# Fourteen opening matmuls, a last tile in three column pieces, and a re-ordered front of a linear-attention and channel-mix kernel

## The chip, the cores and the metric

The kernel runs on one core of a Trainium2 chip. The metric is the time on the device in microseconds (us) of one execution. Before the change it is 198.37 us, the median of three runs (198.21 to 198.51).

## What is computed

Eight batches of 576 tokens with 8 heads of 64 channels go through linear attention without a softmax, an RMS norm per head, and then a channel mix with two gates. The shapes are batch 8, 512 channels, and a hidden width of 1024.

```python
kv = einsum('bhsd,bhse->bhde', k, v)
y = einsum('bhsd,bhde->bhse', q, kv)
y = y / sqrt(mean(y*y, -1) + 1e-6) * g_norm
x = y.transpose(0, 2, 1, 3).reshape(B, S, H * D)
x_prev = x shifted by one token, zero at the first
xk = mu_k * x + (1 - mu_k) * x_prev
xr = mu_r * x + (1 - mu_r) * x_prev
k = max(xk @ w_k, 0)
out = sigmoid(xr @ w_r) * ((k * k) @ w_v)
```

Inputs and output are float32. The kernel works in bfloat16 on TensorE and accumulates in float32.

## The kernel before

The program is a list of steps, the string `ORDER` (lines 18 to 109), which a loop at the end of the kernel (line 685) walks word by word. Each word names a step and its arguments; every step issues its instructions at once to the engines that it uses. Each engine then works through its own instructions in that order, and waits where data or a buffer is not ready. So the order of `ORDER` is the order on every engine and on every DMA queue. A number behind `=` is the PSUM bank that the step's result takes; a mark `'` puts a step on VectorE (DVE) instead of ScalarE (ACT).

The steps that matter here:

- `wm.N` (line 252) issues N matmuls of zeros with 512 columns, whose result nobody reads. `wm.12` and `wm.7` open the program: 19 of them run before any other matmul. Shorter ones (`wm.1`, `wm.2`) stand between the front's steps.
- `lraw`, `lf`, `lw`, `ld` load. `lraw` (first two head pairs of k and v of batch 0) goes over SyncE's queue (SP), the others over the GpSimd queue (POOL), one behind the other: q of batch 0, the remaining k and v, q of batch 1, the four quarters of `w_k` (`lw.0.0` to `lw.0.3`), `w_r`, k and v of batch 1, two halves of `w_v`, and then the later batches. POOL issues a load only when the eighth load before it has landed.
- `cast` turns the raw k and v into bfloat16. `kc` (line 301) multiplies k with v for two batches with 64x64 matmuls; `kco` copies a product out of PSUM. `qc` (line 312) transposes q on TensorE, `qco` copies it out. `uc` (line 323) multiplies the transposed q with the product.
- `sq` squares on ACT (line 434), `ms` averages with a matmul (line 438), `rs` takes the reciprocal root on ACT (line 443), `mu` multiplies on DVE (line 462). That is the norm. `col` transposes the small vectors mu_k, mu_r and g_norm.
- `dc`, `sc`, `add`, `fu` blend x with the token before it.
- `Kf`, `Kl` (lines 530 and 541) are batch 0's matmuls with `w_k`, `Kfo`, `Klo`, `ksp` the relu and the square behind them. `K`, `Ko`, `ks` are the same for the later batches (line 555).
- `R` and `S` are the matmuls with `w_r` (line 575) and the sigmoid; `V` those with `w_v` (line 585), `fin` the last product on DVE (line 600), `st` the store on SP's queue (line 617).
- `tab` (line 647) loads ACT's table, either for the reciprocal root or for the sigmoid; a load blocks ACT.

The last tile, tile 8 of batch 7, has 128 tokens and 512 columns. `L.1` and `L.0` (line 593) compute its right and its left half of columns with eight matmuls each, `Lf` multiplies with the sigmoid on DVE, and `Ls` stores. Each half of columns is stored as two DMAs of 64 tokens: one on SP's queue and one on ACT's.

```python
    def store_half(n, part):
        ...
        (nc.sync, nc.scalar)[n].dma_start(out=dst[half(n), c], in_=o[half(n)])
```

At the end of the program SP waits, in nine instructions one behind the other, for the semaphores of all DMAs (each store's semaphore is one of eight that are given out in turn) before the engines meet and the kernel ends.

Of the kernel before, what the change touches and what calls it, by code (L numbers as in the profile page):

```python
# [21 lines left out]
    sq.0.0 col.1 qco.0.2.192.576' ms.0.1=2 rs.0.1 mu.0.1 qc.0.0.2.0.192=70 qco.0.0.0.192 ms.0.0=1 rs.0.0 mu.0.0  # L22
    kc.0.2.3=3 kco.0.2 wm.2=2 uc.0.2=2 sq.0.2 qco.0.3.192.576 lf.0.1.3.4.0.576 dc.0.0.2.256.576 lf.0.0.3.4.0.576
    kc.0.3.4=7 kco.0.3 wm.1=1 ms.0.2=1 rs.0.2 wm.1=6 uc.0.3=6 sq.0.3 uc.0.4=3 sq.0.4 sc.0.0.0.256.576'
    sc.0.0.1.256.576' qco.0.1.0.192' wm.1=5 uc.0.6=5 sq.0.6 add.0.0.0.256.576 mu.0.2 ms.0.3=4 rs.0.3 mu.0.3
    ms.0.4=7 rs.0.4 mu.0.4 wrap.0 uc.0.5=0 sq.0.5 ms.0.6=1 rs.0.6 dc.0.2.3.256.576 lf.1.2.0.4.0.576 wm.2=2
    qc.1.0.2.0.576=24 qco.1.1.0.576 qc.1.2.4.0.576=76 qco.1.3.0.576 fu.0.0.2.256.576 mu.0.6 dc.0.3.4.256.576
    ms.0.5=3 rs.0.5 qco.1.2.0.576 tab.1.0 fu.0.0.3.256.576 mu.0.5 dc.0.0.4.0.256 sc.0.0.0.0.256 sc.0.0.1.0.256
    lw.0.0.0.4.0.2 Kf.1.0.2.256=1 Kf.0.0.2.256=4 Kf.0.2.3.256 qco.1.0.0.576' lw.0.1.0.4.2.4 wm.2=6
    Kf.3.0.2.256=6 Kf.2.0.2.256=5 Kf.2.2.3.256 Kf.2.3.4.256 Kf.3.2.3.256 Kf.3.3.4.256 sc.0.1.0' sc.0.1.1'  # L30
    add.0.0.0.0.256 Kf.0.3.4.256 Kfo.0.256 lw.0.2.0.4.4.6 Kf.5.0.4.256=3 sc.0.0.3.0.256' Kfo.5.256
    Kf.4.0.4.256=7 lw.0.3.0.4.6.8 sc.0.1.2 Kf.6.0.4.256=0 Kf.7.0.4.256=2 sc.0.0.2.0.256' Kfo.6.256
    add.0.0.1.0.256 Kf.1.2.3.256 Kl.0.256=4 Kl.2.256=3 Klo.2.256 Kfo.7.256 sc.0.1.3' Kfo.4.256 lw.1.0.0.4.0.4
    lf.1.0.0.4.0.576 add.0.1.0 add.0.1.1 lf.1.1.0.2.0.576 R.0.2=0 S.0.2 Klo.0.256 Kf.1.3.4.256 ksp.4.8.256.576'
    R.0.3=3 S.0.3 Kfo.1.256' Kfo.2.256 Kfo.3.256' ksp.0.4.256.576' lf.1.1.2.4.0.576 R.0.1=2 S.0.1 R.0.0=7 S.0.0
# [77 lines left out]
def kernel(  # L113
# [605 lines left out]
```

## Time and profile before

| | us |
|---|---|
| median of three runs | 198.37 |
| range of the three runs | 198.21 to 198.51 |
| the profiled execution | 198.81 |
| its span, first to last instruction | 197.0 |
| TensorE (PE) busy, matmuls | 189.2, 96% of the span |
| ACT busy | 153.4, 78% |
| DVE busy | 150.0, 76% |

The page of the profile gives busy time of each engine, a chain of waits that follows the work back from the last instruction, the costliest groups of instructions, and the DMA issues with their median time to landing. PE's weight loads (PEld) run beside its matmuls. Matmuls overlap: a matmul's own duration is longer than its distance to the next one, so costs on PE are best taken from starts. In the timeline a bracket behind a row says how long the engine sat idle before it and what ended the wait. The DMA engines are busy at a share of 0.9 or more in nearly every slice of the first third of the span, and later more loosely.

### The profile page before, as it was taken

The page shows a single profiled execution, that of the slowest core. Times are in us where ns is not written, and L with a number is a line of the kernel's source. Part 1 is how long each engine was busy: PE and PEld are TensorE (multiplying, and loading weights), DVE is VectorE, ACT ScalarE, POOL GpSimd, SP SyncE. Part 2 cuts the span into 40 slices and gives each one's busy share as a digit, 9 for nine tenths or more (in the row PEclk, how much of TensorE's full clock was granted, in tenths as well). Part 3 has the DMA queues.
Part 4 walks back from the last instruction along what each step waited for, and adds up shares of the span by engine and source line. Part 5 has one row for each costly group of instructions (what it writes and reads, how often), then busy time and mean ns, then how long its engine had stood idle before and what let it go on. Part 6 is the DMA issues. An engine that isn't in the chain of part 4 may idle for free.

```text
span 197.0 us, 4744 instructions
## 1 busy us (share of the span) xinstructions
PE 189.2 (96%) x1879; PEld 111.4 (57%) x1900; DVE 150.0 (76%) x331; ACT 153.4 (78%) x297; POOL 33.2 (17%) x54
## 2 busy tenths in 40 slices
PE   7989999999999999999999999999999999999991
PEld 2445754447744566456754667546854586476451
DVE  4177957894998778984989778897897898779141
ACT  3389799887688799999998978998699877267810
POOL 7864431000390000520090000000000000000000
PEclk9999999999999999999999999999999999999999
DMA  6999999999699999899979995982530426006053
GB/s 218 214 204 197 204 206 207 206 193 198 116 172 232 207 201 168 178 220 201 189 122 245 194 198 106 200 260 89 130 101 0 161 53 194 25 0 237 32 160 106
DMA packets 49035, 32.24 MB, mean 164 GB/s; under 512 B 25324, under 2 KB 44020, under 8 KB 49012
## 3 DMA queue, kind: packets, MB, share of 16 engines
q0 software_dynamic: 22160, 16.19, 54.9%
q1 hardware_dynamic: 26692, 15.61, 32.9%
q8 instruction: 15, 0.25, 0.5%
q10 hardware_dynamic: 160, 0.13, 0.3%
q14 instruction: 8, 0.07, 0.1%
HBM read 33.56 MB, written 9.44 MB: 218 GB/s over the span
## 4 chain that ended last, share of the span: by engine, by line
PE 85%; DVE 6%; ACT 6%; issue 1%; ACTq 0%
PE ps_v L585 28%; PE ps_km L555 24%; PE ps_r L575 15%; PE ps_warm L252 4%; PE ps_ms L438 3%; PE ps_km L530 2%; DVE xT L462 2%; PE ps_km L541 1%; PE ps_u L391 1%; PE ps_u L323 1%; ACT sq L434 1%; ACT L647 1%; ACT sig L580 1%; PE ps_kv L337 1%; PE ps_v L593 1%
## 5 line engine op out<-in xcount | busy, mean ns | idle before, releaser
L585 PE MATMUL ps_v<-wv_sb,sqk 128*128 128x512 bf16 x269 | 63.1, 379 | 0.5
L555 PE MATMUL ps_km<-xk,wk_sb 128*128 128x288 bf16 x448 | 61.0, 286 | 0.0
L555 PEld LDWEIGHTS <-wk_sb 128*128 128x128 bf16 x448 | 42.9, 98 | 14.7 <-issue 1.0
L585 PEld LDWEIGHTS <-sqk 128*128 128x128 bf16 x280 | 27.0, 98 | 30.5 <-ACT sqk L523 1.2
L519 DVE TENSOR_SCALAR rt<-ps_km 128x288 bf16<-128x288 f32 (+2 forms) x61 | 26.4, 460 | 10.1 <-PE ps_km L555 8.8
L575 PE MATMUL ps_r<-wr_sb,xr 128*128 128x512 bf16 x137 | 32.8, 379 | 0.5 <-DVE m L501 0.2
L600 DVE TENSOR_TENSOR out_sb<-ps_v,sig 128x512 f32<-128x512 f32 (+1 forms) x37 | 24.6, 671 | 10.0 <-PE ps_v L585 4.4
L517 ACT ACTIVATE rt<-ps_km 128x288 bf16<-128x288 f32 (+2 forms) x63 | 24.6, 419 | 8.8 <-PE ps_km L555 7.0
L499 ACT ACTIVATE m<-dx,cols 128x576 bf16<-128x576 bf16 (+1 forms) x32 | 22.4, 750 | 4.6 <-DVE dx L490 2.9
L580 ACT ACTIVATE sig<-ps_r 128x512 bf16<-128x512 f32 x36 | 20.7, 607 | 4.9 <-PE ps_r L575 4.6
L523 ACT ACTIVATE sqk<-rt 128x576 bf16<-128x576 bf16 (+1 forms) x33 | 22.3, 691 | 1.6 <-DVE rt L519 1.4
L575 PEld LDWEIGHTS <-xr 128*128 128x128 bf16 x144 | 14.0, 98 | 15.5 <-DVE xr L510 0.2
L462 DVE SCALAR_TENSOR_TENSOR xT<-ps_u,cols,rs 128x512 bf16<-128x512 f32 (+4 forms) x31 | 19.0, 626 | 3.7 <-ACT rs L443 3.4
L443 ACT ACTIVATE rs<-ps_ms,eps 128x512 f32<-128x512 f32 (+4 forms) x31 | 18.0, 593 | 3.9 <-PE ps_ms L438 3.6
L647 ACT ACT_TABLE_LOAD x15 | 19.2, 1283 | 0.3
L434 ACT ACTIVATE sq<-ps_u 128x512 bf16<-128x512 f32 (+4 forms) x31 | 14.6, 502 | 1.1 <-PE ps_u L323 1.0
L525 DVE TENSOR_TENSOR sqk<-rt 128x576 bf16<-128x576 bf16 (+2 forms) x27 | 12.9, 491 | 2.8 <-ACT rt L517 2.3
L366 POOL COPY gates<-qT 128x1 bf16<-128x1 bf16 x5 | 1.5, 305 | 74.1 <-DMA qT<-in_q 74.1
L510 DVE TENSOR_TENSOR xr<-m,xT 128x1152 bf16<-128x1152 bf16 x16 | 11.6, 752 | 1.6 <-ACT m L499 1.5
L510 DVE TENSOR_TENSOR xk<-m,xT 128x1152 bf16<-128x1152 bf16 (+2 forms) x17 | 11.7, 698 | 0.6 <-ACT m L499 0.5
L252 PE MATMUL ps_warm<-zeros 128*128 128x512 bf16 x27 | 10.0, 503 | 1.4 <-DVE eps L259 1.2
L501 DVE TENSOR_SCALAR m<-dx,cols 128x576 bf16<-128x576 bf16 (+2 forms) x34 | 10.9, 358 | 0.2
(80 smaller groups left out, 172.3 us busy)
## 6 DMA issues: line engine op xcount, KB each, us to landing
out_dram<-out_sb SPq DMA_DIRECT2D x23, 256.0 KB, 2.8
in_k<-in_k_dram POOLq DMA_DIRECT2D x7, 576.0 KB, 13.9
in_v<-in_v_dram POOLq DMA_DIRECT2D x6, 576.0 KB, 11.7
in_q<-in_q_dram POOLq DMA_DIRECT2D x6, 512.0 KB, 16.2
out_dram<-out_sb SPq DMA_DIRECT2D x24, 128.0 KB, 2.8
wk_sb<-in_moe_w_k_dram POOLq DMA_DIRECT2D x4, 256.0 KB, 10.6
wv_sb<-in_moe_w_v_dram POOLq DMA_DIRECT2D x2, 512.0 KB, 15.1
sqk<-in_v_dram SPq DMA_DIRECT2D x1, 576.0 KB, 3.7
```

The source lines that it names most:

```text
L462: DVE.scalar_tensor_tensor(out=dst, in0=ps, scalar=g_sb, in1=rs, op0=ALU.mult, op1=ALU.mult)
L499: eng.activation(out=out_, in_=in_, func=AF.Copy, scale=mu)
L510: DVE.tensor_add(out=blended(a, which)[:, hs, c0:c1], in0=at[a]["m", which][:, hs, c0:c1], in1=xT[a % 2][:, hs, P + c0:P + c1])
L517: eng.activation(out=dst, in_=ps, func=AF.Relu)
L519: eng.tensor_scalar(out=dst, in0=ps, scalar1=0.0, scalar2=None, op0=ALU.max)
L523: eng.activation(out=dst, in_=src, func=AF.Square)
L555: nc.tensor.matmul(ps, wk_sb[:, cc, 128 * fc:128 * fc + 128], at[b]["xk"][:, cc, SH * h:SH * h + SH], start=(cc == 0), stop=(cc == NHP - 1))
L575: nc.tensor.matmul(ps, xr[:, cc, 128 * t:128 * t + 128], wr_sb[:, cc, :], start=(cc == 0), stop=(cc == NHP - 1))
L580: ACT.activation(out=sig[b, t], in_=give(("r", b, t)), func=AF.Sigmoid)
L585: nc.tensor.matmul(ps, sqk[:, fc, 128 * t:128 * t + 128], wv_sb[:, fc, :], start=(fc == 0), stop=(fc == NFC - 1))
L600: DVE.tensor_mul(out=o, in0=give(("v",) + key), in1=sig[b, t][:, c])
L647: "tab": lambda eng, n, b: ACT.preload_act_table_set(("abs_reciprocal_sqrt_and_small", "sigmoid_and_others")[n]),
```

## The change

Three things change.

1. The program opens with `wm.14` instead of `wm.12` and `wm.7`.
2. The front's steps, down to the products of batch 2, stand in another order. `kc.0.0.2` now stands ahead of the transposes of q, `col.0` moves back behind the first `uc`; many copies move between ACT and DVE (batch 1's four `kco` are now all on DVE); the third quarter of `w_k` is loaded before the second; batch 1's first half of v is loaded before its k; `uc.1.0` to `uc.1.4` stand together. Short `wm` steps stand at other places. Behind the front the order is the old one with the PSUM banks renamed.
3. The last tile is computed in three pieces of columns: 256 to 511 (`L.1`), 0 to 127 (`L.0`), 128 to 255 (`L.2`). Each piece is stored with one DMA of all 128 tokens, the first and the last on SP's queue, the middle one on ACT's.

The diff, with the long list cut to the front's beginning, the place of batch 1's products and the end:

```diff
-    set.0 set.2 lraw.1 lraw.0 lrow wm.12=0 lf.0.2.0.2.0.576 lf.0.2.2.4.0.576 lf.0.0.2.3.0.576 lf.0.1.2.3.0.576
-    set.1 wm.7=1 col.0=1 cast.1 cast.0' qc.0.0.2.192.576=23 qco.0.1.192.576 kc.0.0.2=45 kco.0.1 kco.0.0' wm.2=6
-    uc.0.1=6 qc.0.2.4.0.192=70 qco.0.2.0.192' qco.0.3.0.192' qc.0.2.4.192.576=34 qco.0.0.192.576 sq.0.1 uc.0.0=5
+    set.0 set.2 lraw.1 lraw.0 lrow wm.14=0 lf.0.2.0.2.0.576 lf.0.2.2.4.0.576 lf.0.0.2.3.0.576 lf.0.1.2.3.0.576
+    set.1 cast.1 cast.0' kc.0.0.2=12 kco.0.0 qc.0.0.2.0.192=34 qco.0.1.0.192' kco.0.1' qc.0.0.2.192.576=56
+    qco.0.0.192.576' wm.2=7 uc.0.0=7 qco.0.0.0.192 qco.0.1.192.576' col.0=0 uc.0.1=1 qc.0.2.4.0.192=43
...
-    lw.0.0.0.4.0.2 Kf.1.0.2.256=1 Kf.0.0.2.256=4 Kf.0.2.3.256 qco.1.0.0.576' lw.0.1.0.4.2.4 wm.2=6
-    Kf.3.0.2.256=6 Kf.2.0.2.256=5 Kf.2.2.3.256 Kf.2.3.4.256 Kf.3.2.3.256 Kf.3.3.4.256 sc.0.1.0' sc.0.1.1'
...
-    tab.0.1 Kl.1.256=0 kc.1.0.2=41 kco.1.0' kco.1.1' Klo.1.256' kc.1.2.4=36 kco.1.2 uc.1.0=5 sq.1.0
-    ksp.0.4.0.256' uc.1.4=2 sq.1.4 uc.1.2=7 sq.1.2 Kl.3.256=4 Klo.3.256' kco.1.3 ms.1.4=1 rs.1.4 mu.1.4 ms.1.0=0
-    rs.1.0 mu.1.0 uc.1.1=3 sq.1.1 ms.1.2=6 rs.1.2 mu.1.2 lw.2.0.0.4.0.4 V.0.1.0=1 uc.1.5=4 uc.1.3=2 sq.1.3
...
+    qc.1.2.4.0.576=72 qco.1.1.0.576 qco.1.3.0.576 lw.0.0.0.4.0.2 Kf.1.0.2.256=6 wrap.0 mu.0.6 dc.0.0.4.0.256
+    sc.0.1.0 sc.0.1.3' qco.1.2.0.576' Kf.0.0.2.256=1 Kf.1.2.3.256 Kf.0.2.3.256 lw.0.2.0.4.4.6 sc.0.1.1' wm.1=0
+    Kf.5.0.4.256=0 Kf.4.0.4.256=5 Kfo.4.256' sc.0.0.3.0.256 Kf.0.3.4.256 Kfo.0.256 sc.0.0.1.0.256'
+    lw.0.1.0.4.2.4 Kf.2.0.2.256=3 Kf.3.0.2.256=2 Kf.2.2.3.256 Kf.2.3.4.256 Kf.3.2.3.256 lw.0.3.0.4.6.8 wm.1=7
+    Kf.7.0.4.256=7 sc.0.0.0.0.256' sc.0.0.2.0.256' add.0.0.0.0.256 Kf.3.3.4.256 Kf.6.0.4.256=5 Kf.1.3.4.256
...
+    R.0.2=6 R.0.0=3 Kl.1.256=7 ksp.0.4.256.576' lf.1.0.0.4.0.576 Klo.2.256' kc.1.0.2=52 ksp.4.8.256.576'
+    kco.1.0' lf.1.1.2.4.0.576 kc.1.2.4=40 uc.1.0=5 kco.1.1' uc.1.1=2 S.0.2 kco.1.2' uc.1.4=6 uc.1.2=4 kco.1.3'
+    uc.1.3=0 Klo.0.256 S.0.0 tab.0.1 Klo.1.256' ksp.0.4.0.256' sq.1.0 ms.1.0=1 sq.1.4 ms.1.4=3 sq.1.2 rs.1.4
...
-    S.7.5 fin.7.5 st.7.5 fin.7.6 st.7.6 L.1=7 Lf.1 Ls.0.1 Ls.1.1 L.0=4 Lf.0 Ls.0.0 Ls.1.0
+    S.7.5 fin.7.5 st.7.5 fin.7.6 st.7.6 L.1=3 Lf.1 Ls.0.1 L.0=7 Lf.0 Ls.1.0 L.2=5 Lf.2' Ls.0.2
...
+    LAST = (slice(0, C // 4), slice(C // 2, C), slice(C // 4, C // 2))
+
     def last_vv(part):
 
-        c = slice(C // 2 * part, C // 2 * part + C // 2)
+        c = LAST[part]
...
-    def store_half(n, part):
+    def store_last(n, part):
         o = outs[B - 1, 8, part]
         dst = rows_of(B - 1, 8)[0][1]
-        c = slice(C // 2 * part, C // 2 * part + C // 2)
-        (nc.sync, nc.scalar)[n].dma_start(out=dst[half(n), c], in_=o[half(n)])
+        (nc.sync, nc.scalar)[n].dma_start(out=dst[:, LAST[part]], in_=o)
```

More of the change, by code (lines that the diff above doesn't have):

```diff
@@ L24 @@
[L24 to L28, printed above, removed]
@@ new lines @@
+    set.1 cast.1 cast.0' kc.0.0.2=12 kco.0.0 qc.0.0.2.0.192=34 qco.0.1.0.192' kco.0.1' qc.0.0.2.192.576=56
+    qco.0.0.192.576' wm.2=7 uc.0.0=7 qco.0.0.0.192 qco.0.1.192.576' col.0=0 uc.0.1=1 qc.0.2.4.0.192=43
+    qco.0.3.0.192' qc.0.2.4.192.576=25 qco.0.2.192.576' qco.0.3.192.576' sq.0.1 ms.0.1=6 sq.0.0 ms.0.0=3
+    qco.0.2.0.192' col.1 rs.0.1 mu.0.1 kc.0.2.3=2 kco.0.2 wm.1=5 uc.0.2=5 uc.0.5=4 rs.0.0 mu.0.0 sq.0.2
+    lf.0.0.3.4.0.576 lf.0.1.3.4.0.576 kc.0.3.4=0 kco.0.3 dc.0.0.2.256.576 sc.0.0.0.256.576' sq.0.5 wm.2=6
@@ new lines @@
+    lw.2.1.4.8.0.4 V.0.2.1 ksp.4.8.0.256 tab.1.1 mu.1.3 wrap.1 dc.1.0.2.0.576 V.0.3.0=5 V.0.3.1 dc.1.2.4.0.576
+    sc.1.1.0 sc.1.1.1' V.0.0.1 sc.1.1.3' V.0.1.1 sc.1.1.2 add.1.1.0 add.1.1.1 R.1.6=2 fin.0.3 ld.0.2 R.1.8=4
+    sc.1.0.0 sc.1.0.3 sc.1.0.2 sc.1.0.1' add.1.0.0 ld.1.2 R.1.4=1 S.1.4 fin.0.1 add.1.0.1 kv.2=05 K.1.2.1=6
+    K.1.2.0=1 fin.0.0 kvo.2.0 fin.0.2 Ko.1.2.0 kvo.2.1' ld.2.2 kvo.2.3 K.1.3.0=3 kvo.2.2' K.1.6.0=7 K.1.5.0=0
+    ld.2.3 S.1.8 K.1.1.0=1 Ko.1.1.0 S.1.6 K.1.6.1=5 R.1.7=4 K.1.5.1=1 S.1.7 Ko.1.2.1' kvo.2.5' Ko.1.3.0
@@ new lines @@
+    K.1.1.1=6 Ko.1.5.0 Ko.1.5.1' R.1.5=2 S.1.5 K.1.0.0=4 K.1.0.1=3 K.1.4.0=1 K.1.4.1=0 Ko.1.6.0 kvo.2.4' qd.2.0
+    u.2.0=27 Ko.1.6.1 tab.0.2 sq.2.1 Ko.1.1.1' ks.1.1' Ko.1.0.0' ks.1.5' Ko.1.0.1' ks.1.0 Ko.1.4.0' qd.3.0
+    Ko.1.4.1' ks.1.2' ks.1.4' u.2.1=64 sq.2.2 K.1.3.1=5 Ko.1.3.1' ks.1.3' K.1.7.0=3 ks.1.6 qd.2.1 K.1.7.1=1
+    Ko.1.7.0' st.0.3 qd.3.1 st.0.0 Ko.1.7.1' ks.1.7' ms.2.1=0 gt.2 gt.3 rs.2.1 mu.2.1 ld.1.3 ld.0.3 V.1.7.0=5
+    st.0.1 V.1.7.1 fin.1.7 sq.2.3 ms.2.3=3 u.2.2=1 sq.2.0 rs.2.3 ms.2.0=0 rs.2.0 ms.2.2=7 rs.2.2 V.1.6.0=5
@@ new lines @@
+    V.1.5.0=3 V.1.5.1 ld.1.4 mu.2.3 sq.2.4 ms.2.4=0 ld.0.4 V.1.8.0=4 V.1.8.1 rs.2.4 mu.2.0 tab.1.2 V.1.4.0=7
+    V.1.6.1 V.1.4.1 mu.2.2 d.2.0 d.2.1 d.2.4 ld.1.5 mu.2.4 d.2.2 d.2.3 sc.2.1.0 sc.2.1.2 sc.2.0.0 sc.2.0.1
+    sc.2.0.3 ld.2.4 ld.0.5 sc.2.1.3' sc.2.1.1' add.2.1.0 add.2.1.1 R.2.3=2 R.2.1=6 S.2.1 R.2.0=0 kv.3=16 fin.1.6
+    sc.2.0.2' add.2.0.0 fin.1.4 add.2.0.1 fin.1.8 qd.4.0 gt.4 kvo.3.3' K.2.5.0=5 R.2.2=7 kvo.3.2' K.2.0.0=4
+    Ko.2.0.0' S.2.0 st.0.2 qd.4.1 S.2.3 kvo.3.1 kvo.3.0 kvo.3.5 kvo.3.4 K.2.0.1=0 K.2.2.0=2 S.2.2 tab.0.3
@@ new lines @@
+    fin.1.5 st.1.5 zl Ko.2.2.0' Ko.2.0.1' u.3.1=61 sq.3.2 sq.3.3 K.2.3.0=7 ks.2.0 K.2.1.0=4 Ko.2.3.0' st.1.6
+    K.2.5.1=3 Ko.2.5.0' ms.3.3=2 K.2.1.1=0 rs.3.3 Ko.2.5.1' ms.3.2=7 rs.3.2 Ko.2.1.0' Ko.2.1.1' mu.3.2 ld.0.6
+    K.2.2.1=5 ks.2.1 Ko.2.2.1 ld.2.5 u.3.2=3 kv.4=42 u.3.0=07 K.2.3.1=6 mu.3.3 K.2.6.1=5 kvo.4.3' ld.1.6 sq.3.4
+    kvo.4.2' qd.5.0 gt.5 kvo.4.0' sq.3.0 ms.3.0=1 sq.3.1 kvo.4.1' Ko.2.3.1 ks.2.5' rs.3.0 ks.2.2' K.2.7.1=2
+    ms.3.1=4 rs.3.1 K.2.7.0=6 Ko.2.7.0 Ko.2.7.1' mu.3.0 K.2.4.1=1 K.2.6.0=2 ks.2.3' kvo.4.5 ks.2.7 mu.3.1
@@ new lines @@
+    ms.3.4=4 rs.3.4 Ko.2.6.0 K.2.4.0=6 Ko.2.4.0' Ko.2.4.1 ks.2.4 Ko.2.6.1 ks.2.6 d.3.0 d.3.4 mu.3.4 V.2.0.0=0
+    d.3.1 d.3.2 V.2.3.0=7 sc.3.0.0' sc.3.1.0 sc.3.1.2 st.1.7 V.2.1.0=4 V.2.1.1 qd.5.1 kvo.4.4 sc.3.1.3'
+    sc.3.0.3' sc.3.1.1 sc.3.0.2 fin.2.1 st.1.8 st.2.1 add.3.1.1 V.2.0.1 fin.2.0 V.2.3.1 kv.5=26 kvo.5.3 kvo.5.0
+    u.4.1=15 u.4.0=34 kvo.5.2 st.1.4 add.3.1.0 tab.1.3 R.3.7=0 sc.3.0.1' fin.2.3 kvo.5.1 R.3.6=6 S.3.6 sq.4.1
+    R.3.5=7 S.3.5 sq.4.2 S.3.7 add.3.0.0 ld.1.7 ld.0.7 ld.2.6 R.3.4=2 S.3.4 add.3.0.1 K.3.3.0=6 R.3.8=7 S.3.8
@@ new lines @@
+    tab.0.4 Ko.3.3.0' K.3.3.1=0 Ko.3.3.1' K.3.5.0=6 K.3.5.1=2 Ko.3.5.0' Ko.3.5.1' ms.4.1=7 rs.4.1 K.3.1.0=0
+    K.3.2.0=6 Ko.3.2.0' Ko.3.1.0 K.3.7.0=2 Ko.3.7.0' K.3.7.1=7 Ko.3.7.1' sq.4.3 sq.4.0 ms.4.2=0 rs.4.2 K.3.2.1=6
+    ms.4.3=2 K.3.6.0=7 K.3.6.1=0 mu.4.1 Ko.3.2.1' ks.3.2' rs.4.3 mu.4.3 K.3.1.1=4 kvo.5.4 Ko.3.6.0' Ko.3.6.1
+    ks.3.6' Ko.3.1.1 ks.3.7 ms.4.0=6 ld.2.7 K.3.4.0=2 mu.4.2 K.3.0.0=0 Ko.3.0.0 ks.3.1' ks.3.3 K.3.0.1=5
+    Ko.3.0.1 ks.3.0' rs.4.0 mu.4.0 kvr.5.1' u.4.2=4 kv.6=70 kvo.6.3' sq.4.4 V.2.2.0=1 ks.3.5 Ko.3.4.0 V.2.2.1
@@ new lines @@
+    d.4.0 kvo.5.5 fin.2.2 ms.4.4=5 K.3.4.1=6 rs.4.4 mu.4.4 d.4.4 Ko.3.4.1 kvo.6.0 d.4.1 d.4.2 ks.3.4 d.4.3
+    sc.4.1.0 sc.4.0.0' V.3.6.0=3 sc.4.1.3' V.3.7.0=2 qd.6.0 gt.6 V.3.7.1 sc.4.1.1' fin.3.7 add.4.1.0 sc.4.1.2
+    sc.4.0.1 add.4.1.1 kvo.6.1 V.3.5.0=5 ut.5.1=6 add.4.0.0 sc.4.0.2 V.3.6.1 fin.3.6 V.3.5.1 tab.1.4 sc.4.0.3'
+    fin.3.5 R.4.1=1 S.4.1 add.4.0.1 R.4.3=4 kvo.6.5 ut.5.0=2 sqt.5.0 rdt.5.0 kvr.6.0' R.4.0=7 S.4.0 S.4.3
+    sqt.5.1 rdt.5.1 K.4.3.0=3 R.4.2=1 S.4.2 kvo.6.2 K.4.5.0=5 K.4.3.1=7 Ko.4.3.0' K.4.4.0=4 Ko.4.3.1' tab.0.5
@@ new lines @@
+    K.6.4.0=1 Ko.6.4.0 mut.7.0 rdt.7.2 st.4.3 mut.7.1 K.6.7.0=3 rdt.7.3 rst.7.1 mut.7.2 Ko.6.7.0 mut.7.3
+    K.6.7.1=0 Ko.6.7.1' K.6.2.1=7 K.6.1.0=1 Ko.6.1.0 Ko.6.1.1 K.6.5.0=6 Ko.6.5.0' Ko.6.2.1' K.6.0.0=3 Ko.6.0.0'
+    qd.7.1 ur.7=1 ks.6.1 ks.6.7 sq.7.4 K.6.4.1=2 K.6.0.1=5 Ko.6.0.1' st.5.7 K.6.3.0=4 Ko.6.3.0 K.6.3.1=0
+    Ko.6.3.1' st.4.0 st.5.6 ks.6.3' ks.6.0 K.6.5.1=6 Ko.6.5.1' ks.6.5' ms.7.4=7 rs.7.4 K.6.6.0=3 mu.7.4 ks.6.2
+    K.6.6.1=4 yd.7.1 Ko.6.6.0' Ko.6.4.1 yd.7.0 V.6.1.0=5 Ko.6.6.1 V.6.3.0=0 yd.7.2 gs.7.0 ks.6.6' yd.7.3 gs.7.1
@@ new lines @@
+    d.7.0 d.7.1 d.7.4 V.6.0.0=7 ks.6.4 d.7.2 sc.7.0.0 sc.7.0.1' sc.7.0.3 sc.7.0.2' V.6.2.0=6 V.6.3.1 add.7.0.0
+    add.7.0.1 V.6.0.1 V.6.2.1 V.6.1.1 K.7.6.0=2 Ko.7.6.0 K.7.1.0=1 Ko.7.1.0 K.7.1.1=4 Ko.7.1.1' fin.6.0
+    K.7.7.1=3 K.7.7.0=2 K.7.5.0=1 st.5.5 st.5.8 fin.6.1 K.7.5.1=4 Ko.7.5.0' Ko.7.7.0 Ko.7.7.1' sc.7.1.0'
+    sc.7.1.1 st.4.2 sc.7.1.2 Ko.7.5.1' K.7.3.1=7 ks.7.5 K.7.0.1=2 add.7.1.0 fin.6.2 K.7.2.0=5 st.6.2 K.7.6.1=1
+    Ko.7.6.1 Ko.7.2.0 sc.7.1.3 ks.7.1 st.6.1 st.6.0 K.7.4.0=3 Ko.7.4.0' fin.6.3 add.7.1.1 K.7.3.0=4 Ko.7.3.0
```

110 lines of the change are left out of this document (32 added, 78 removed).

## The prediction

> **What bounds the kernel.** I read the page first, then the chain of waits, then the timeline of the first 48 us and of the last ten, then the DMA issues.
>
> ```profile
> span 197.0 us, 4744 instructions
> PE 189.2 (96%) x1879; PEld 111.4 (57%) x1900; DVE 150.0 (76%) x331; ACT 153.4 (78%) x297; POOL 33.2 (17%) x54
> ```
>
> PE is busy 96% of the span, so time comes out only where PE stands or works for nothing: the first 17 us, small holes after that, and the last 4 us, in which PE is done.
>
> The chain (start, length, what):
>
> ```profile
> 1.20 7.06 PE ps_warm L252 x19
> ...
> 19.01 3.69 PE ps_km L530 x26
> ...
> 28.22 0.60 ACT sig L580
> 28.83 1.28 ACT L647
> 30.12 0.22 ACT kvc L245
> 30.39 0.43 PE ps_u L323 x4
> ...
> 105.32 0.22 PE ps_u L391 x4
> ...
> 191.13 1.93 PE ps_v L593 x16
> 193.08 0.42 DVE out_sb L600
> ```
>
> The 19 zero matmuls run alone to 8.26. Near 30 us the chain leaves PE: batch 1's `u` waits for a copy of `kvc` that stands on ACT behind a sigmoid and a 1.28 us table load. At the end stand 16 half-width matmuls and one product on DVE.
>
> The timeline, for the pace of the zero matmuls (their weight loads) and for POOL, whose next load waits until an older one has landed:
>
> ```profile
> 6.29 0.15 PEld L252 LDWEIGHTS <-zeros 128*128 128x128 bf16 x1 [0.28 <-issue]
> 6.72 1.04 PEld L252 LDWEIGHTS <-zeros 128*128 128x128 bf16 x5 [0.28 <-issue]
> ...
> 16.12 0.72 POOL L199 DMA_DIRECT2D in_v<-in_v_dram  x1 [3.29 <-DMA q<-in_q_dram]
> 17.31 0.76 POOL L220 DMA_DIRECT2D wv_sb<-in_moe_w_v_dram  x1 [0.47 <-DMA wk_sb<-in_moe_w_k_dram]
> ...
> 21.31 0.74 POOL L199 DMA_DIRECT2D in_v<-in_v_dram  x1 [0.57 <-DMA wk_sb<-in_moe_w_k_dram]
> ...
> 29.56 0.69 POOL L213 DMA_DIRECT2D in_qr<-in_q_dram  x1 [0.53 <-DMA in_v<-in_v_dram]
> ```
>
> Up to the fourteenth the matmuls come 0.427 us apart, from the fifteenth (7.01) 0.216: the granted clock doubles about 5.7 us after the first. The brackets date landings within 0.3 us: q of batch 1 near 16, the first quarter of w_k near 17.1, its last near 21.1, batch 1's last half of v near 29.3. The DMA engines are busy throughout, so another order on PE moves none of these.
>
> **Beginning.** Five full-rate matmuls go: 5 x 0.216 = 1.08 us, so PE reaches real work at 7.18 instead of 8.26. `kc.0.0.2` is ready: the two casts end at 5.65 and 6.68. `col` no longer stands ahead of the transposes. But the first `Kf` (17.50 before) needs the w_k quarter of 17.1 and stands behind the 72 transposes of batch 1's q, 0.82 us that cannot begin before 16. I place it near 17.4 and take the 1.08 us at nothing. The cover is these loads; were they earlier, up to 1.1 us more would come.
>
> From there to `R`: behind the landing of the last quarter (21.1) the new order has one zero matmul (0.2), ten `Kf` of 0.138 (1.4) and 16 `Kl` of 0.118 (1.9), which gives 24.6. Before, `R` began at 24.43, with one `Kf` left for later. The exchange of quarters two and three, equal in size, moves `Kf` with it; POOL's queue is as long as before. So `R` is 0.15 later, bounds -0.3 to +0.3.
>
> **Batch 1.** 16 `R` (3.45) and eight `Kl` (0.95) end near 29.0. `kc.1.2.4` needs the half of v that lands near 29.3 in both orders, since v and k ahead of it only change places. Here both stand level again. Before, the first `V` started at 32.57. From 29.45 the old order streams 2.43 us up to it: the products 0.31, four `u` 0.70, `Kl.3` 0.95, three means 0.48. PE turns three times between 64x64 and whole-array matmuls. A turn costs 0.095 (a 288-column matmul at 47.125 streams 0.1225, the products start at 47.341). That makes 2.72; 0.4 is standing, the wait for ACT's copy. In the new order the four copies are on DVE (0.22 each), behind neither sigmoid nor table load, and the five `u` stand together, so that those of pairs 2 and 3 use different quarters of the array at once. That this works is seen at 52.07, where 16 matmuls of 256 columns in four quarters take 0.56. The stream is 2.5, one turn 0.1, and a remaining wait 0.15: `V` at 32.2, 0.35 earlier. `uc.1.3` (0.215) is then already done, which before stood between the `V`. Together -0.55; writing both orders out step by step (each starts when its engine is free and its inputs are there, durations from the trace; for the old order the starts fall within 0.3 us of the trace up to 48 us) gives -0.5. I take -0.5, bounds 0 (DVE, 9.07 of 11 us busy from 17 to 28, brings a copy late) and -0.8.
>
> **Middle.** From 48 to 191 us the order is unchanged, banks are only renamed, and PE has almost no hole: the 0.5 us is carried through, unless a load stops it. The nearest one seen is v of batch 6, landing at 95.7 for products at 98.4, so it isn't.
>
> **End.** PE now streams eight matmuls of 256 columns (0.109 each) and 16 of 128. The row of 128 columns in the chain (L391, four in 0.22) gives 0.0555 each, 16 make 0.89 where eight of 256 made 0.87: +0.01. The last product shrinks: 0.69 for 512 columns, 0.42 for 256, so 0.29 for 128, -0.13.
>
> The stores, by the last issue's row:
>
> ```profile
> out_dram<-out_sb SPq DMA_DIRECT2D x1, 64.0 KB, 2.2
> out_dram<-out_sb ACTq DMA_DIRECT2D x1, 64.0 KB, 2.5
> ```
>
> 64 KB in 64 rows of 1 KB take 2.2 on SP and 2.5 on ACT. The new last piece is again 64 KB, in 128 rows of 512 bytes. Its bounds are 2.1 and the 2.8 of the 256 KB stores with 128 rows; I take 2.3, as the bytes are the same: +0.1. ACT's only store now is the middle piece, 0.4 us earlier, and falls out of the end. SP's store of the right half is issued some 0.7 us ahead of the last, longer than an issue takes there (0.47), so nothing queues.
>
> Then SP's closing waits:
>
> ```profile
> L714 SPq EVENT_SEMAPHORE  x8: 27/28/28, 195.7 to 196.1; - x8
> ```
>
> The last SP store held the semaphore that is asked for second of nine, so eight waits of 0.06 followed its landing. One DMA fewer shifts the turn: the last store now holds the one asked for last. Seven waits go under cover: 7 x 0.062 = -0.43. If the landing came later than SP's, this would be smaller, hence 0 to -0.43.
>
> **Sum**, against the profiled execution (198.81, span 197.04, so 1.77 around it): -0.5 + 0.01 - 0.13 + 0.1 - 0.43 = -0.95, rounded to -0.9 because the bounds of the landing lean to later. The span becomes 196.1, that execution 197.9. The median of three runs lies 0.44 lower than the profiled one: 198.37 - 0.9 = 197.5.
>
> **A rule against the end.** The Trainium skill, page "TensorE: Matmul & The Clock Gate", section "Back-to-back issue gap", gives about 81 ns for each matmul of 128 columns in a stream with weight loads, and 131 ns for 512. By that the 16 would take 1.30, 0.4 us more than here, and the time would be 197.9, an estimate from that page. The trace shows 55 ns (L391) and 216 ns at 512 columns, so it does not agree.
>
> **Rivals.** (a) Only the end pays: `V` of batch 1 comes no earlier, because DVE delivers the copies late or `R` waits for `xr`. For it: DVE's load there. Against: the copies are short and stand ahead of longer steps. 198.37 - 0.4 = 197.95.
>
> (b) Only the front pays: the short rows land after 2.7 us, and the end is worth nothing, 198.37 - 0.5 = 197.9. Or the narrow matmuls are held to the 98 ns of their weight loads (the mean of line 585's): 16 x 0.098 = 1.57, 0.7 more, 198.15. Against this stands L391, whose loads follow each other at 55 ns.
>
> (c) The clock, slower than before. The rise to 0.216 was seen only behind fourteen matmuls, the number that is now left. If it needed the five, PE would run the front at half rate. From 7.2 to 17.3 the 13 remaining zero matmuls alone would take 13 x 0.21 = 2.7 us more and the real ones some 2, of which about 1.7 fit into holes and behind the weights. The loss is 3, the time 198.37 - 0.9 + 3 = 200.5. It decides when the rise comes after about 10.3 us: until 8.5 the weights hide it, at 10.3 it eats the 0.9. Against: the fifteenth was fast at 7.01 though the work up to there is what stays, and now products, transposes and two zero matmuls follow without a hole to 8.5.
>
> The Trainium skill, same page, section "What's actually happening", has the clock rise after a free-running window of some 3.4 us kept busy, at a moment that differs from run to run. By that a run whose window ends after 7.2 depends on the small matmuls counting as work; 14 would mostly do. The 5.7 us seen here agrees with a window that had begun too early to count; no run here shows another phase.
>
> (d) The 1.08 us does pay in full, because transposes or w_k are not what holds `Kf`: 196.4. Against: the brackets at 16.12 and 17.31.
>
> **Chances.** Forecast 0.62; (a) 0.12; (b) 0.10; (c) 0.08; (d) 0.03; another late engine of the front, some 0.5 slower, 0.05. A measurement of this kernel can tell about 0.2%, 0.4 us, from no change. (a) and (b) lie on that line and are split: faster 0.62 + 0.11 + 0.03, about 0.77; same 0.13; slower 0.10. The range takes in (a), (b), the front's bounds and the scatter of 0.15 between runs: 197.0 to 198.2.
>
> **What would show it.** Right: the products of line 301 start near 7.2 at full rate; first `Kf` near 17.4; `R` near 24.6; no row of ACT `kvc` near 30 in the chain; `V` at 32.2; the 16 matmuls of 128 columns in 0.9; last product's end near 192.9; last landing near 195.2, with two or fewer closing waits behind it; span 196.1. Wrong: zero matmuls 0.427 apart after 8 us, `R` later than 24.9, PE at 48 us less than 0.3 earlier, or a last landing over 2.5 us after its issue.

## The result and the profile after

The changed kernel takes 197.56 us (median of five runs, 197.44 to 197.68), the kernel before, beside it, 198.40 (198.21 to 198.92). The ratio is 0.9947, 95% interval 0.9931 to 0.9964; here and below the ratio is an estimate over all executions and can differ from the quotient of the two medians, which is 0.9958 here. The forecast was 197.5. The profiled execution of the changed kernel took 197.44, the one of the kernel before 198.81: the pair of profiles is 1.37 apart where the medians are 0.84 apart, so a part of what the two traces show is scatter and must be told from the change.

The page of the changed kernel, its first lines:

```profile
span 195.7 us, 4772 instructions
PE 189.7 (97%) x1905; PEld 111.3 (57%) x1905; DVE 153.9 (79%) x341; ACT 150.8 (77%) x288; POOL 32.7 (17%) x54
```

PE is busy as long as before in a span 1.4 us shorter: what went is time in which PE stood, was done, or multiplied zeros. (The kernel before lacks some matmul records, 269 of the 280 on one line, so the two busy times are alike only roughly.)

The timeline at the beginning (the zero matmuls, DVE's cast, and the first products with their weight loads; a bracket says what ended the idle time before a row):

```profile
1.20 5.65 PE L252 MATMUL ps_warm<-zeros 128*128 128x512 bf16 x14 [1.20 <-DVE eps L259]
...
5.96 0.76 DVE L247 CAST rt<-sqk 128x1152 bf16<-128x1152 f32 x1 [2.64 <-DMA sqk<-in_k_dram]
6.26 0.10 PEld L252 LDWEIGHTS <-zeros 128*128 128x128 bf16 x1 [0.24 <-issue]
6.78 0.37 PEld L301 LDWEIGHTS <-rt 64*64 64x64 bf16 x36 [0.42 <-DVE rt L247]
6.78 0.48 PE L301 MATMUL ps_kv<-rt 64*64 64x64 bf16 x36
```

The granted clock doubles at 6.20 us, and the last zero matmul starts at 6.47. The first products start at 6.78, just behind the end of DVE's cast (6.72). The 0.42 us in the bracket is idle time of the weight loads only; PE itself stands for less than 0.1 us there.

The chain of waits between `R` and the first `V`, and at the end:

```profile
24.36 2.60 PE ps_r L575 x12
...
26.99 0.60 ACT sig L580
...
28.07 0.49 ACT sig L580
...
28.58 1.28 ACT L648
...
29.93 0.60 ACT sq L434
...
30.57 0.43 PE ps_ms L438 x2
31.00 0.87 PE ps_km L541 x8
...
32.09 0.86 PE ps_v L585 x4
...
190.41 1.78 PE ps_v L595 x24
...
192.22 0.29 DVE out_sb L602
```

The copy of `kvc` on ACT (30.12 before) is gone from the chain, but the chain has not left ACT: sigmoid, table load and the first square still stand one behind the other. At the end the last product is 0.29 instead of 0.42.

The DMA issues with their size and time to landing, and the closing waits between 194.6 and 194.82 (their number, the length of one in ns, and the first and last start):

```profile
out_dram<-out_sb ACTq DMA_DIRECT2D x1, 64.0 KB, 2.5
out_dram<-out_sb SPq DMA_DIRECT2D x1, 64.0 KB, 2.2
```

```profile
L715 SPq EVENT_SEMAPHORE  x2: 28/28/28, 194.6 to 194.8; - x2
```

Two waits are left there, one for each of the last two stores; where eight followed the landing before, the last store's wait is now the last of all.

To tell scatter from change I cut every trace at five events: the start of the first `R`, of the first `V`, of the first `u` of batch 2 (L381), the end of the last matmul, and the end of the span. The differences, in us, from those starts and ends:

| kernel | first R | R to V | V to L381 | to the last matmul's end | to the span's end |
|---|---|---|---|---|---|
| before | 24.43 | 8.14 | 19.51 | 140.97 | 4.00 |
| before, second profile | 24.54 | 8.14 | 19.51 | 140.98 | 3.98 |
| new end alone | 24.53 | 8.14 | 19.51 | 141.12 | 3.45 |
| before, 14 zero matmuls | 23.90 | 8.14 | 19.51 | 140.86 | 4.00 |
| changed | 24.20 | 7.73 | 19.27 | 140.98 | 3.48 |
| changed, second profile | 24.36 | 7.81 | 19.27 | 140.85 | 3.45 |
| new front alone | 24.30 | 7.74 | 19.27 | 140.85 | 3.98 |
| changed, one more store | 24.20 | 7.75 | 19.27 | 140.88 | 3.92 |

`R` to `V`, `V` to L381 and the end follow the program and hardly scatter here. The start of `R` and the middle do: `R` by 0.6 in the old order, the middle by 0.27 over both.

### The profile page after: what moved, and what is told of

It reads as the page before. It is cut to its first block, busy times and chain, and to the rows that moved or that the text cites. A ratio compares the mean times of both kernels' runs of the same rounds, so it can differ in the third digit from the quotient of the medians.

```text
span 195.7 us, 4772 instructions
## 1 busy us (share of the span) xinstructions
PE 189.7 (97%) x1905; PEld 111.3 (57%) x1905; DVE 153.9 (79%) x341; ACT 150.8 (77%) x288; POOL 32.7 (17%) x54
## 4 chain that ended last, share of the span: by engine, by line
PE 88%; ACT 5%; DMA 3%; issue 1%; DVE 1%; ACTq 0%; POOLq 0%
PE ps_v L585 31%; PE ps_km L555 27%; PE ps_r L575 15%; PE ps_ms L438 3%; DMA q<-in_q_dram 3%; PE ps_km L530 3%; PE ps_kv L337 2%; PE ps_u L391 1%; ACT sig L580 1%; PE ps_km L541 1%; ACT sq L434 1%; ACT L648 1%; PE ps_warm L252 1%; PE ps_v L595 1%; PE ps_u L323 1%
## 5 line engine op out<-in xcount | busy, mean ns | idle before, releaser
L585 PE MATMUL ps_v<-wv_sb,sqk 128*128 128x512 bf16 x280 | 63.9, 379 | 0.0
L519 DVE TENSOR_SCALAR rt<-ps_km 128x288 bf16<-128x288 f32 (+2 forms) x66 | 28.9, 465 | 10.9 <-PE ps_km L555 10.2
L575 PE MATMUL ps_r<-wr_sb,xr 128*128 128x512 bf16 x144 | 33.5, 379 | 0.0
L602 DVE TENSOR_TENSOR out_sb<-ps_v,sig 128x512 f32<-128x512 f32 (+2 forms) x38 | 24.7, 658 | 9.7 <-PE ps_v L585 5.4
L517 ACT ACTIVATE rt<-ps_km 128x288 bf16<-128x288 f32 (+2 forms) x58 | 22.4, 414 | 7.4 <-PE ps_km L555 6.4
L501 DVE TENSOR_SCALAR m<-dx,cols 128x576 bf16<-128x576 bf16 (+2 forms) x34 | 11.4, 369 | 0.3
```

What stands on the lines that cost most here:

```text
L517: eng.activation(out=dst, in_=ps, func=AF.Relu)
L519: eng.tensor_scalar(out=dst, in0=ps, scalar1=0.0, scalar2=None, op0=ALU.max)
L575: nc.tensor.matmul(ps, xr[:, cc, 128 * t:128 * t + 128], wr_sb[:, cc, :], start=(cc == 0), stop=(cc == NHP - 1))
L585: nc.tensor.matmul(ps, sqk[:, fc, 128 * t:128 * t + 128], wv_sb[:, fc, :], start=(fc == 0), stop=(fc == NFC - 1))
L602: DVE.tensor_mul(out=o, in0=give(("v",) + key), in1=sig[b, t][:, c])
```

## Experiments

The kernel before ran beside the experiments in four groups, with medians of 198.60, 198.37, 198.63 and 198.71; each ratio is to the executions of the same group. "The rise" below is the moment from which the full clock was granted.

**The new end alone** (the kernel before with `LAST`, `store_last` and this list):

```diff
-    ... L.1=7 Lf.1 Ls.0.1 Ls.1.1 L.0=4 Lf.0 Ls.0.0 Ls.1.0
+    ... L.1=7 Lf.1 Ls.0.1 L.0=4 Lf.0 Ls.1.0 L.2=2 Lf.2' Ls.0.2
```

> The old front with the new end. Theory (the prediction's terms): the end pays +0.01 - 0.13 + 0.1 - 0.43 = -0.45 us against the kernel before, so about 197.95, ratio 0.9977; the last store's wait is the last of the closing waits, and the span ends about 0.95 us behind the last landing instead of 1.36. Rival 1, the end is worth nothing because the store in 128 rows of 512 bytes lands later: 198.4. Rival 2, the end carries the whole gain: 197.55, ratio 0.996. PE's steps up to 190 us should start within 0.3 us of those of the kernel before.

Measured: 198.32 (197.61 to 199.24), before 198.60, ratio 0.9976 (0.9957 to 0.9995). From the last matmul's end to the span's end it takes 3.45 us, 0.54 less than in the old end; the lowest time is 0.54 lower too (197.61 against 198.15). The theory's ratio of 0.9977 is met. The medians differ by only 0.28, and the ratio's interval reaches from 0.1 to 0.85 us, so the size of the gain rests on the trace.

**The new front alone** (the order list of the changed kernel, pieces and stores of the old end):

```diff
-    ... L.1=3 Lf.1 Ls.0.1 L.0=7 Lf.0 Ls.1.0 L.2=5 Lf.2' Ls.0.2
+    ... L.1=3 Lf.1 Ls.0.1 Ls.1.1 L.0=7 Lf.0 Ls.0.0 Ls.1.0
```

> The new front with the old end (two pieces, two stores of the last). Theory: -0.5 us against the kernel before, about 197.9, ratio 0.9975, with the first V of batch 1 near 32.0 and the first u of batch 2 (line 381) near 51.3; behind the last landing stand eight closing waits again. Rival, the trace's -0.87 us on PE is all the order's: 197.5, ratio 0.9955. Rival, the front only moved with the loads, which landed 0.27 us earlier in that one profile: 198.3 or more. If the two halves add up, the gains of this run and of the tail alone make 0.8.

Measured: 197.99 (197.80 to 198.73), ratio 0.9968 (0.9952 to 0.9984). The two ratios multiply to 0.9944; the whole change gave 0.9947 and, measured again, 0.9961. So the halves add up within the scatter, the end with some 0.5 us and the front with some 0.6.

**One more store** (the changed kernel; the store of tile 5 of batch 7 goes as two DMAs of 64 rows):

```diff
-    S.7.5 fin.7.5 st.7.5 fin.7.6 ...
+    S.7.5 fin.7.5 sth.7.5 fin.7.6 ...
+        for i in range(2):
+            nc.sync.dma_start(out=dst[half(i)], in_=o[half(i)])
```

> The changed kernel, with the store of tile 5 of batch 7 split into two transfers of 64 rows on SP's queue, so that the last store holds the semaphore that is asked for early again. Theory (turn of the closing waits): PE and the last landing stay as they are, seven or eight waits of 0.062 us follow the landing, and the time is 0.43 us longer than the changed kernel's: 198.0, ratio to the kernel before 0.998. Rival, the end's gain comes from the landing or the shorter product alone: 197.55, ratio 0.996.

Measured: 198.12 (197.79 to 198.61), ratio 0.9967 (0.9952 to 0.9982). The closing waits between 194.6 and 195.17 in its trace:

```profile
L721 SPq EVENT_SEMAPHORE  x8: 27/28/28, 194.7 to 195.1; - x8
```

Eight waits again. The landing comes 2.23 us after the last issue, as in the changed kernel (2.22), but the span ends 1.33 us behind it instead of 0.92. That is 0.41 for the turn of the semaphores, shown by a DMA that does no other harm: the stretches ahead of the landing are those of the changed kernel within 0.1 us.

**14 zero matmuls in the old order:**

```diff
-    set.1 wm.7=1 col.0=1 cast.1 cast.0' ...
+    set.1 wm.2=1 col.0=1 cast.1 cast.0' ...
```

> The kernel before with 14 zero matmuls at the beginning instead of 19, and nothing else. Theory: the loads hold the first Kf, so the 1.08 us of five full-rate matmuls are worth 0 to -0.2 us: 198.2 to 198.4, ratio 0.999 to 1.000; the first Kf starts at 17.2 to 17.5, though the first real matmul comes about 1 us earlier. Rival (d): it pays in full, 197.3, ratio 0.9945. Rival (c): the clock rises later without the five and the front runs at half rate, 1 us or more slower. Third: where the rise comes late in a run, the 19 at half rate reach past 8.5 us and push the first Kf; then the time's scatter between runs (198.21 to 198.92 before) shrinks to some 0.3 us and the median falls by up to 0.3.

Measured: 198.32 (198.17 to 198.93), before 198.60, ratio 0.9986 (0.9971 to 1.0002); the lowest times are alike (198.17 and 198.15). The timeline of PE at the transposes of batch 1's q and the first `Kf`, of the kernel before:

```profile
16.57 0.82 PE L312 MATMUL ps_qt<-ident,q 64*64 64x64 bf16 x72
...
17.50 0.76 PE L530 MATMUL ps_km<-xk,wk_sb 128*128 128x320 bf16 x4
```

and with 14 zero matmuls:

```profile
15.93 0.82 PE L312 MATMUL ps_qt<-ident,q 64*64 64x64 bf16 x72
...
16.86 0.89 PE L530 MATMUL ps_km<-xk,wk_sb 128*128 128x320 bf16 x5
```

q landed at 15.83 and 15.40. In the profiled execution before, the transposes started 0.74 behind the landing: PE was late, not the load. The first `Kf` starts 0.64 earlier here, as do the transposes. The rise of the clock decides: it came at 6.87 there and at 4.41 here. In the profile of the new end alone, which has the old front and its rise at 7.07, `Kf` started at 17.60, though its weights had landed at 16.68. In the second profile of the kernel before it came at 4.13, and with all 19 zero matmuls the first real matmul started at 7.57, as with 14 (7.53). So the five matmuls are free where the clock rises early and cost up to 0.6 where it rises late. The expectation's first and third theory are both half right: the median fell by 0.28, but the times still spread from 198.17 to 198.93. That the five pay 1.08 is refuted.

**Both kernels again,** unchanged:

> The changed kernel, unchanged, for its scatter beside the others and a second profile. In the profiles so far the granted clock rose at 4.4 to 7.1 us, another moment in each; the tail alone was worth -0.54 us by the lowest times and -0.28 by the medians, the front alone -0.35 and -0.61. If the halves add up: lowest time near 197.3, median near 197.7, and the front as in the first profile (first V near 31.9) wherever the rise falls before 8 us.

> The kernel before, unchanged, for a second profile. Theory (the clock's phase): where the granted clock rises by about 5 us, the first Kf starts at 16.9 to 17.1 behind the weights and the first V near 32.0, as in the kernel with 14 zero matmuls, and the time is near 198.2; where it rises at 6.9 or later, Kf starts at 17.5 or later and the time is 198.6 or more. Rival: the front stands at 17.5 and 32.57 whatever the clock does, and the scatter comes from elsewhere.

Measured: changed 197.65 (197.41 to 197.86), ratio 0.9961 (0.9947 to 0.9975); before 198.49 (198.18 to 200.33). The changed kernel kept its front with a rise at 7.18: first `V` at 32.16 (31.93 in the first profile). For the kernel before, the expected theory of the clock's phase (the moment of the rise) failed as stated. The clock rose at 4.13 and `Kf` started at 16.98, yet the time was 198.94: the last quarter of w_k landed at 21.51, 1.88 behind the third (1.31 in the first profile), and `R` began at 24.54. Loads scatter as well as the clock, and either can set `R`.

**19 zero matmuls in the new order:**

```diff
-    set.0 set.2 lraw.1 lraw.0 lrow wm.14=0 ...
+    set.0 set.2 lraw.1 lraw.0 lrow wm.19=0 ...
```

> The changed kernel with 19 zero matmuls at the beginning. By the prediction's term they cost nothing, since loads hold the first Kf: same as the changed kernel. By the reading of the experiments so far the new order has no slack there (its transposes of batch 1's q start within 0.6 us of the landing): PE's steps to Kf come 1.08 us later and less than half of that hides, the time is 0.3 to 0.9 us longer, more where the clock rises late: median near 198.3, ratio to the changed kernel 1.003.

Measured: 197.74 (197.34 to 198.36), against 197.65 for the changed kernel beside it. Its profiled execution, the slowest of the eight, had the rise at 6.16, as in the first profile of the changed kernel (6.20): first `Kf` 17.72 against 17.08, `R` 24.83 against 24.20, time 198.36 against 197.44. Of the rest, 0.13 lies between `V` and L381 (19.40, the one exception to 19.27 in the new order) and 0.14 in the middle. With the rise at the same moment the five cost 0.6 in `R`; over all runs only some 0.1, within the scatter. The expected 198.3 was too much.

**9 and 11 zero matmuls in the new order** (the same edit, `wm.9` and `wm.11`):

> The changed kernel with 9 zero matmuls at the beginning. Theory (the clock rises at a moment of its own window, and what PE has to do up to 8 us keeps it busy enough): the same as the changed kernel within 0.1 us, or up to 0.1 lower. Rival (c) of the prediction, the rise needs the zero matmuls: the granted clock rises 3 us or more later in some or all executions, the front runs at half rate behind 8.5 us, and the time is 0.5 us or more longer in those.

> The changed kernel with 11 zero matmuls at the beginning. With 9 PE stood 1.56 us between the zero matmuls and the first product, and the granted clock, risen at 5.06 us, fell back at 8.47 and rose for good at 15.30; with 14 and 19 no such fall was seen. With 11 the zero matmuls end at 5.2 to 5.9 us, and PE stands 0.9 to 1.5 us. Theory (a stretch of about 3.4 us is judged by how long PE stood in it): some executions fall and take 199.2 or more, the others take 197.4 to 197.8; the mean clock tells them apart (0.98 against 0.995 and above). Rival, what counts is the number of zero matmuls and 11 still do: all within 197.4 to 197.9.

With 9: 199.56 (198.22 to 200.92), ratio 1.0056 (1.0033 to 1.0079). The busy time by stretches of its trace (stretch, length, then busy time of PE, PEld, DVE, ACT and POOL with counts, granted clock, DMA share, GB/s) and a row of PE's timeline:

```profile
5.00:8.50 3.50, 1.54 (x75) 0.88 (x76) 1.56 (x5) 1.19 (x3) 3.50 (x5) 1.00 1.20 223
8.50:15.30 6.80, 6.25 (x95) 3.41 (x98) 4.04 (x13) 3.77 (x10) 3.69 (x6) 0.50 1.25 203
```

```profile
6.76 0.48 PE L301 MATMUL ps_kv<-rt 64*64 64x64 bf16 x36 [1.56 <-DVE rt L247]
```

PE stood 1.56 us before the first products. The clock had risen at 5.06; after a stretch in which PE was busy 1.54 of 3.50 us it fell to half at 8.47, 3.41 behind the rise, and came back at 15.30. `R` starts at 25.92, 1.7 later than in the changed kernel. This is rival (c) of the prediction at work, five zero matmuls further on than the change goes.

With 11: 197.86 (197.55 to 199.55), three of ten runs at 198.68 or more. The profile is one of these: the clock did not fall, it rose late, at 10.56. One such window of 3.41 earlier, at 7.15, it had not risen, and in the 3.41 before that PE had stood 1.1 us. `R` starts at 25.32, 1.1 later than in the changed kernel. The mixture was expected; that the mean clock would tell the runs apart was not borne out, since that mean (1.000 here) leaves out the time ahead of the first rise.

**Copies of `kvc`, two ways.** In the new order the copies 2 and 3 go to ACT, behind the table load:

```diff
-    ... S.0.2 kco.1.2' uc.1.4=6 uc.1.2=4 kco.1.3' uc.1.3=0 Klo.0.256 S.0.0 tab.0.1
+    ... S.0.2 Klo.0.256 S.0.0 tab.0.1 kco.1.2 uc.1.4=6 uc.1.2=4 kco.1.3 uc.1.3=0
```

> The changed kernel with the copies of kvc 2 and 3 of batch 1 on ACT behind the sigmoid and the table load, where the kernel before has them; everything else as changed. The prediction's batch-1 term: this copy is most of the -0.5 (0.4 of it a standing PE). Written out step by step: the first V 0.15 to 0.2 us later than in the changed kernel (32.1 to 32.2), the time 0.2 longer, median near 197.8. Rival, the gain of batch 1 lies in the order of u and means alone: 0. Rival, ACT's table load costs all of it: 0.5 or more, 198.1.

In the old order they go to DVE, ahead of its other work:

```diff
-    ... kco.1.1' Klo.1.256' kc.1.2.4=36 kco.1.2 uc.1.0=5 ... Klo.3.256' kco.1.3
+    ... kco.1.1' kc.1.2.4=36 kco.1.2' kco.1.3' Klo.1.256' uc.1.0=5 ... Klo.3.256'
```

> The kernel before with only the copies of kvc 2 and 3 of batch 1 moved to DVE, ahead of its other work; the old order of u, means and V stays. The measure is the stretch from the first R to the first V, which was 8.14 us in four profiles of the old order, 7.73 to 7.80 in five of the new one and 7.92 in the new one with these copies on ACT. The prediction's step (0.4 us of PE standing for ACT's copy): the stretch falls to 7.75, the median by 0.4, ratio 0.998. Theory now: the squares stand behind ACT's table load whoever makes the copy, and the copy is worth 0.05 to 0.2: the stretch 7.95 to 8.1, the ratio 0.999 to 1.000. Rival, nothing or a loss, as DVE's later steps move back: 8.14 or more.

New order, copies on ACT: 197.77 (197.53 to 198.03), ratio 0.9942 (0.9920 to 0.9964). That is not distinguishable from the changed kernel, which did not run beside it. The trace is clearer. `R` to `V` takes 7.91 instead of 7.73 to 7.81, and the chain of waits says why:

```profile
28.85 1.28 ACT L648
30.13 0.02 ACTq L434
30.15 0.32 ACT kvc L245 x2
30.47 0.51 ACT sq L434
```

The copies stand between the table load and the first square. Measured from the end of the table load, the first `V` comes 2.45 us later in four profiles of the old order, 2.07 in seven of the new one (2.14 in an eighth) and 2.25 here. The table load itself ends 5.66 to 5.69 behind the first `R` in both orders. So the copy is worth 0.18 of the 0.38.

Old order, copies on DVE: 198.61 (198.15 to 199.12), before 198.71, ratio 0.9987 (0.9973 to 1.0001); `R` to `V` 8.25, longer than the 8.14. This execution can't judge the copy: v landed at 29.35 and held the second half of the products until 29.39, when the table load was over at 29.82. The ratio's interval excludes neither nothing nor the prediction's 0.4. The trace does show that with `R` at 24.13 v is what comes last, so that an earlier `R` would bring nothing there.

**A version meant to beat both,** without the single zero matmuls at 15, 18 and 21 us:

```diff
-    ... lf.1.2.0.4.0.576 wm.1=6 ... sc.0.1.1' wm.1=0 ... lw.0.3.0.4.6.8 wm.1=7
+    ... lf.1.2.0.4.0.576 ... sc.0.1.1' ... lw.0.3.0.4.6.8
```

> A version that may beat both: the changed kernel without the single zero matmuls that stand at 15, 18 and 21 us between the transposes of batch 1's q and the Kf. In the changed kernel the first Kf starts 0.17 to 0.80 us behind the first quarter of w_k's landing. Theory, PE and not the load holds Kf and R there: the first Kf 0.1 to 0.4 us earlier, R up to 0.4 earlier, the first V up to 0.35 earlier (the load of batch 1's last half of v takes over), the time 0 to 0.3 us shorter, median near 197.45. Rival, the loads hold it: 0. Rival, the zero matmuls are needed for the clock there: it falls between 15 and 25 us and the time is 0.5 or more longer.

Measured: 197.74 (197.22 to 198.67), ratio 0.9950 (0.9932 to 0.9968). The lowest time is the lowest of all, the median isn't better than the changed kernel's. In the profile the three places read, on PE's timeline:

```profile
17.02 0.99 PE L530 MATMUL ps_km<-xk,wk_sb 128*128 128x320 bf16 x6 [0.20 <-DMA wk_sb<-in_moe_w_k_dram]
18.40 2.45 PE L530 MATMUL ps_km<-xk,wk_sb 128*128 128x320 bf16 x16 [0.39 <-DMA wk_sb<-in_moe_w_k_dram]
21.50 1.53 PE L530 MATMUL ps_km<-xk,wk_sb 128*128 128x320 bf16 x10 [0.65 <-DMA wk_sb<-in_moe_w_k_dram]
```

Each wait now names a quarter of w_k. The zero matmuls had filled time that the loads take anyway; the clock held at full rate through these gaps. The longest wait is long in part because this execution's last quarter landed 1.78 behind the third, where the changed kernel's took 1.31. The expected median of 197.45 was not met.

## Why the prediction was right, step by step

**The sum.** Forecast -0.9, measured -0.84 by the medians. Between the two profiled executions it was -1.37: by the table, `R` -0.23, `R` to `V` -0.41, `V` to L381 -0.24, the middle +0.01, the end -0.52 (to the rounding). Both profiled executions of the kernel before (198.81 and 198.94) lie above its medians, both of the changed kernel (197.44 and 197.50) below its own, so the pair of traces shows too much. Setting the sum against the median, 0.44 below the profiled execution, was what kept the forecast from following one late front. The three stretches that follow the program sum to -1.17; the medians fell by 0.84 and, measured again, by 0.72, the lowest times by 0.77 both times. So some 0.3 to 0.5 must come back ahead of `R` or in the middle. That the forecast lies within 0.06 is in part luck: `R` to `V` was taken 0.13 too large, the end 0.07 too small, and the +0.15 for `R` is small beside what comes back.

**The end, -0.45 predicted.** From the last matmul's end: the product is 0.13 shorter, as predicted; the landing comes 2.22 behind the issue instead of 2.15, +0.06 where +0.1 was taken; the turn of the closing waits gives -0.44 where -0.43 was predicted (one wait is 0.06). The 24 matmuls take 1.93 from first start to last end, as against 1.91. The 16 of 128 columns follow each other at 0.056. So the page "TensorE: Matmul & The Clock Gate" of the Trainium skill, section "Back-to-back issue gap", with 81 ns for this width, doesn't hold here, and neither does the part of rival (b) with 98 ns. One thing was only touched in this step: in the old end ACT's last store landed at 196.03, 0.34 behind SP's, and its wait was the last of the eight. Had only the turn been changed, that landing would by these figures have kept most of the 0.43; no run tried this. The gain needs ACT's store to become the middle piece as well; it then landed at 194.59, SP's last one at 194.75.

**The beginning: "I take the 1.08 us at nothing".** This step failed in its reason and was small in its effect. The bracket at 16.12 dated the landing of q rightly, but the transposes in the same trace started at 16.57, behind a PE that ran late. The cover was thinner than claimed: in the old order with 19 zero matmuls it was whole where the clock rose at 4.13 and 4.63 us, and some 0.6 showed through where it rose at 6.87 and 7.07. By medians the five are worth 0.1 to 0.3, not separable from zero. In the new order the loads are no cover at all: in all eight profiles that keep its single zero matmuls the first `Kf` starts 1.05 us behind the start of the transposes and `R` 7.12 us behind `Kf`, both within 0.02, and the transposes start at least 0.46 us behind the landing of q. PE's own work sets these times. One likely reason that an earlier start brings so little, tested by no run, is that the new list has 11 zero matmuls between the opening and these transposes where the old one has 9, so that of the five only three, 0.65 us, are saved.

**`R` at 24.6, 0.15 later.** It came at 24.20 and 24.36. Against the old order's best front (23.90, with 14 zero matmuls, in an execution of 198.17) the first of these is later by 0.3, the upper bound; against the two profiles of the kernel before it is 0.1 to 0.3 earlier, but both of those took longer than the median. Set beside the shorter execution, the sign was right and the term too small; this and a middle longer by 0.12 are, in that pair of traces, what comes back of the -1.17. The reason was wrong: `R` does not stand 3.5 us behind the landing of the last quarter. That distance was 3.28 to 5.36 in the eight profiles, while the 7.12 behind `Kf` stayed.

**Batch 1, -0.5 in all.** `R` to `V` shrank by 0.4 (predicted 0.54), and `uc.1.3`, no longer between the `V`, gave 0.24 (predicted 0.215). The place was right, the wait was not: "0.4 is standing, the wait for ACT's copy". The standing belongs to the table load and the squares behind it. The copy holds 0.18 of it, by one trace; the other 0.20 is what is left for the new order of `u`, squares and means, which no run took apart further.

**The middle** carried the front's gain through: from L381 to the last matmul 140.85 to 140.98 in both kernels. Why other executions in the table need up to 0.27 more there stays open.

**The rivals.** That only the end pays, (a), is refuted by the new front alone, and that only the front pays, (b), by the new end alone and, for the closing waits, by the extra store. (c) did not come with 14 zero matmuls (none of the changed kernel's eleven runs is above 197.86), but came with 9 and partly with 11. Its size was judged well: a rise at 10.3 was to eat the 0.9, and one at 10.56 gave 198.68, a time of the kernel before. The margin in zero matmuls was smaller than the text made it look. (d) is refuted by the old order with 14.

## What to carry to other kernels

Cut several traces of the same kernel at the same few events before believing a difference between two: stretches that repeat to 0.01 us belong to the program, those that scatter belonged to loads and clock here. Where a kernel's end waits in a fixed order, as here, look which store holds the semaphore that is asked for last: one DMA more or fewer moved this kernel by 0.4 us. Zero matmuls ahead of the first load are a price paid for the clock; take away only as many as leave no long hole in front of the first real work.

## What the runs showed of the hardware

The moment of the clock's rise is spread over nearly a whole window. In 13 of 14 profiles it fell anywhere from 4.13 to 7.18 us, with the first zero matmul always at 1.20; the late one was at 10.56, and the fall and return with 9 zero matmuls were 3.41 and 10.24 us behind the rise, one and three times 3.41. The Trainium skill, page "TensorE: Matmul & The Clock Gate", section "What's actually happening", gives a free-running window of about 3.4 us, which agrees; the scatter of 500 ns to either side that it names is too small for this kernel. Its section "HAM oscillation — how this bites in real kernels" states as the rule that PE must not idle longer than some 3.4 us. Here a hole of 1.56 us within a window in which PE was busy to 43% (9 zero matmuls) brought the clock down. A window busy to 54% (14 zero matmuls, old order) did not. A rise failed to come after windows busy to 68% (11 zero matmuls) and 75% (the changed kernel's second profile, 0.35 to 3.77 us) and came after one busy to 86% (the second profile of the kernel before). These shares are worked out from the starts and ends of the matmuls in five traces, for windows laid out in steps of 3.41 from the rise, and the limits between them are not measured more closely.
